# Attention, soft MoE and SoLU MLP on one core: combine weights turned four tiles at once, first w_out products in three groups

## The chip, the core and the metric

The kernel runs on one core of a Trainium2 chip. Its time is that of one execution on the device in microseconds (us); the number of a kernel is the median of its runs. A core has a matrix engine (TensorE, PE in the profile; PEld is its weight loads), VectorE (DVE), ScalarE (ACT), GpSimd (POOL) and SyncE (SP), which here issues all transfers to the 16 DMA engines. PSUM is the memory that TensorE writes to, SBUF the main memory on the core.

## The reference

Three stages on 4608 tokens in fp32: attention in chunks of 64 positions, a soft mixture of experts with 8 experts of 4 slots, and an MLP with a SoLU and a normalisation over 1024 features.

```python
scores = scale * np.matmul(q_c, k_c.transpose(0, 1, 2, 4, 3))
...                                  # softmax over the chunk
x = (attn @ v_c)                     # 4608 x 512
logits = x @ phi                     # 4608 x 32
d = softmax(logits, over tokens);  slot_input = d.T @ x
slot_out[e] = np.maximum(slot_input[e] @ w1[e], 0.0) @ w2[e]
c = softmax(logits, over slots);   x = c @ slot_out
h = x @ w_in                         # 4608 x 1024
e = np.exp(h - h_max); solu = h * e / (sum(e) + 1e-09)
ln = (solu - mu) / np.sqrt(var + 1e-06) * g_ln
return ln @ w_out                    # 4608 x 512
```

## The kernel before

The 4608 tokens are 36 tiles of 128. The program has three parts.

From 0 to about 131 us a loop of steps works through attention and the logits tile by tile; the logits of all tiles stay in `lall` (128 tokens x 36 tiles x 32 slots).

From there to about 205 us a list of named operations, `ORDER`, sets the order in which the program is written, and with it the order on each engine's queue: every engine works through its own instructions in that order, each one waiting for what it needs. Behind each name stands a small function (`op("name", "what it depends on")(function)`). `ON_VECTOR` lists the evictions and copies that run on VectorE; the others run on ScalarE. In this part come the softmax over tokens, the expert products (`w1_...` and `w2_...`, and `wc48` to `wc63` for the second half of the experts' w2, L963), the slot outputs turned (`soc`, `soct`, L1023), their product with w_in (`sw0`, `sw1`, L1084, evicted to `xb` by `pev`), and the first output tiles. The expert weights stream in beside this; all transfers stand in SP's queue, the weights in the order of use (L123, L127), and each transfer waits for the one eight before it.

Since x is c times slot_out, the kernel multiplies slot_out by w_in once (32 x 1024) and then needs for a tile only `h_ps` = the combine weights of its 128 tokens times this matrix (`h_mm`, L1272, two products of 512 columns). To keep the accuracy, each operand is split in a high and a low part: `c4T` holds for each tile 128 rows, four groups of 32 slots, the groups being high, low, high, low; `s4` holds the matrix as high, high, low, low (`s4h` casts, `s4l` subtracts).

*Combine weights.* Nine blocks of four tiles: `ch` copies a block of `lall` twice into `cc` (rounded: the high part), `cl` writes the rest beside it (L882), `ct` transposes `cc` in four products, one for each tile (L895, `c_ps`), and `ce` evicts the 128 x 512 result into `c4T` (L383 or L384). The first two tiles do without: `cpc`, `cpt`, `cpe` make fp32 transposes `cP` for them.

*First tiles.* Tile 0 (`f_` names) is handled in halves of 512 columns: `f_h0`, `f_h1` are its products (L1240), `f_m0`, `f_m1`, `f_mm` the maximum (L1206, L1209), `f_sc` a scale (L1143 to L1147), `f_e` the exponential, `f_u` the product u = h * e (L1212), `f_uh` its high part in fp16, `f_T` its transposes on TensorE (L1227), `f_Te` their evictions to `uhT`, and `f_ul` the low part (L1233), which a transposing transfer turns into `ulT` (L1236). Tile 1 has its products in `f_g0`, `f_g1`, a maximum in halves (`f_k0`, `f_k1`, `f_km`) and one exponential `f_E`. From tile 2 on a tile is whole: `Hm` (h_ps), `Hx` the maximum (L1277), `He` scale and exponential, `Av` u (L1153) with uh and its transposing transfer (L1167), `Al` ul and its transfer (L1324), `Aq` and `As` the variance.

*w_out products.* `B(i)` makes a tile's output in 24 products of 512 columns (L1345): eight uhT x w_hi, eight uhT x w_lo, eight ulT x w_hi. `B0` stands behind tile 2's h_ps and needs both halves of uhT and ulT in its list of dependencies.

From tile 2's `B` on, a loop runs over the tiles, 24 products and two h_ps products for each; h_ps has two buffers in PSUM, and tile i's is written once u of tile i - 2 has read its own.

Of the kernel before, what the change touches and what calls it, by code (L numbers as in the profile page):

```python
# [9 lines left out]
F32 = mybir.dt.float32  # L10
F32R = mybir.dt.float32r
# [8 lines left out]
NT = 36  # L20
# [16 lines left out]
ce2 ce4 ch0 ch2 ch3 ch4 ch8 cme he00 rl01 rl11 s4h0  # L37
# [9 lines left out]
cms2 cms6 px2 cms3 ht00 he00 cz1 cms4 w1_011 rl01 w2_000 cms7 ht01 px7 cms0 cz2 cz3 px3 w2_001 cz4 px6 cz5 cms5
px5 he01 w2_010 w2_011 id16 so0 px4 cms1 w1_100 sot0 px0 px1 w1_101 late ch0 cl0 px8 wmt ch2 cl2 cpc wmv ct0 ch1
w1_110 rl10 cl1 ch3 ct1 hi0 hi1 lo0 ht10 hi6 ch4 cl3 ce0 cl4 ct2 ce1 ce2 w1_111 he10 cpt cpe ch5 rl11 ct3 wc48
ht11 hi4 ce3 hi5 lo2 wc49 ct4 hi3 hi7 cl5 lo3 hi2 wc50 ch6 he11 ce4 wc51 cl6 wc52 wc53 ct6 wc54 wc55 ch8 ct5 ce6  # L50
soe0 soc0 wc56 wc57 ch7 soct0 cl7 ct7 ce5 wc58 cl8 wc59 wc60 soce0 ce7 wc61 soc2 ct8 soct2 wc62 wc63 soc3 lo1
# [11 lines left out]
def soft_moe_kernel(ctx: ExitStack, tc, qkT, v1, w12, w64, phi, g_ln, cst, out):  # L63
# [73 lines left out]
    free.extend([w_tile(ring)] * RING)  # L137
# [736 lines left out]
    cc_t = {}  # L874
# [12 lines left out]
    def combine_t(b):
        cc = cc_t[b].bitcast(F32)
        if ps3 is None:
            t = ps2.tile([128, 4, 128], F32, tag="c", name="c_ps")  # L890
        else:
            t = ps3.tile([128, 4, 128], F32, tag="uhT_ps", name="c_ps", bufs=1)
        T["c", b] = t
# [289 lines left out]
    def f_open():  # L1183
# [3 lines left out]
        for t in ("nm0", "nm1", "z0", "z1", "z3"):  # L1187
# [10 lines left out]
            ks=(4, 5, 6, 7, 0, 1, 2, 3),  # L1198
# [5 lines left out]
    def f_max(t, n):  # L1204
        x = F["hs"][n] if t == "nm0" else F["h1"][:, ts(n, 512)]
        nc.vector.tensor_reduce(out=F[t][n], in_=x, axis=AX.X, op=ALU.max, negate=True)  # L1206
# [31 lines left out]
    for n_ in range(2):  # L1238
# [5 lines left out]
        op("f_k%d" % n_, "f_g%d" % n_)(lambda n=n_: f_max("nm1", n))  # L1244
# [11 lines left out]
    op("f_km", "f_k0 f_k1")(lambda: f_min("nm1"))  # L1256
# [32 lines left out]
    op("Hm2", "f_h0 f_h1 f_g0 f_g1 s4l0 s4l1 ce0")(lambda: h_mm(2))  # L1289
# [5 lines left out]
    op("B0", "f_Te0 f_Te1 f_ul0 f_ul1 Hm2")(lambda: B(0))  # L1295
    op("Hm3", "B0 Av1")(lambda: h_mm(3))
# [42 lines left out]
    def B(i):  # L1339
        d = st[i]  # L1340
        o = ps3.tile([128, 512], F32, tag="o", name="o_ps", bufs=3)
        n = 0
        for lt, w in ((d["uhT"], w_hi), (d["uhT"], w_lo), (d["ulT"], w_hi)):
            for fc in d.get("ks", range(8)):
                nc.tensor.matmul(o, lt(fc), w(fc), start=(n == 0), stop=(n == 23))  # L1345
                n += 1
        d["o"] = o
# [105 lines left out]
```

## Time and profile before

| | us |
|---|---|
| median of 3 runs | 414.41 |
| lowest and highest run | 413.31, 415.01 |
| profiled execution, whole | 413.71 |
| its span in the trace | 411.9 |
| TensorE busy | 388.2 (94%) |
| VectorE busy | 324.2 (79%) |
| DMA, mean | 241 GB/s |

The span is what the trace shows of the profiled execution; 1.8 us of it lie around the span. Busy shares are means over three parts with different limits: the DMA engines are full in the weight stretch from about 150 to 188 us, TensorE is full in the loop over the tiles. Of the chain that ended last, 45% are the w_out products at L1345.

### The profile page before, as it was taken

What the parts mean: (1) busy time and instruction counts of PE and PEld (TensorE: products, weight loads), DVE (VectorE), ACT (ScalarE), POOL (GpSimd) and SP (SyncE); (2) the same over time, 40 slices, a digit from 0 to 9 for tenths busy, and PEclk for the clock granted to TensorE, in tenths of its full rate; (3) what the DMA queues carried; (4) which work ended last, traced back from release to release, by engine and by line L of the source; (5) the groups of instructions that cost most, each with busy time, mean ns of one, the idle gap of its engine ahead of it and who ended that gap; (6) DMA issues with size and microseconds to landing.
All of it is one profiled execution on the core that took longest, in us unless ns stands there. A gap on an engine that the chain in (4) does not pass through costs nothing.

```text
span 411.9 us, 10062 instructions
## 1 busy us (share of the span) xinstructions
PE 388.2 (94%) x3761; PEld 217.2 (53%) x3761; DVE 324.2 (79%) x790; ACT 224.6 (55%) x458; POOL 207.2 (50%) x200
## 2 busy tenths in 40 slices
PE   3899999999999899989899999999999999999997
PEld 3667767667766642335344444444444444444445
DVE  2699889989988567673889999988888888888840
ACT  2477777777776522223565555655455554554521
POOL 1477766776768428340025555544554454544430
PEclk9999999999999999999989999999999999999999
DMA  6999999999999999993045767775676665666661
GB/s 216 363 386 371 377 382 386 385 371 387 380 380 352 399 399 407 407 410 142 14 91 116 156 150 166 160 147 132 136 145 153 129 141 134 134 154 143 137 156 53
DMA packets 106884, 99.32 MB, mean 241 GB/s; under 512 B 79188, under 2 KB 79828, under 8 KB 106836
## 3 DMA queue, kind: packets, MB, share of 16 engines
q1 hardware_dynamic: 106832, 98.68, 76.9%
q8 instruction: 30, 0.49, 0.5%
q14 instruction: 22, 0.15, 0.1%
HBM read 70.60 MB, written 9.44 MB: 194 GB/s over the span
## 4 chain that ended last, share of the span: by engine, by line
PE 79%; DVE 8%; DMA 5%; ACT 3%; POOL 2%; issue 2%; SPq 1%; ACTq 0%; DVEq 0%; POOLq 0%
PE o_ps L1345 45%; PE s_ps L249 5%; PE h_ps L1272 4%; PE x_ps L275 3%; PE h_ps L912 3%; PE xt_ps L401 3%; DMA vall<-in_v 2%; PE lt_ps L304 2%; PE h_ps L963 2%; PE pt_ps L392 2%; PE h_ps L949 2%; PE sl_ps L456 1%; DMA raw<-in_w 1%; PE o_ps L1357 1%; DMA cs<-in_cst 1%
## 5 line engine op out<-in xcount | busy, mean ns | idle before, releaser
L1158 POOL TENSOR_SCALAR uh<-u,sc 128x1024 f16<-128x1024 f32 (+1 forms) x35 | 72.1, 2059 | 42.7 <-issue 31.8
L1345 PEld LDWEIGHTS <-uhT 128*128 128x128 f16 x560 | 52.5, 99 | 68.6 <-issue 11.3
L1345 PE MATMUL o_ps<-xb,uhT 128*128 128x512 f16 x280 | 67.5, 385 | 0.0
L1345 PE MATMUL o_ps<-wo,uhT 128*128 128x512 f16 x280 | 66.9, 382 | 0.0
L1345 PE MATMUL o_ps<-xb,ulT 128*128 128x512 f16 x280 | 66.2, 379 | 0.0
L1283 ACT ACTIVATE e<-h_ps,nm 128x1024 f32<-128x1024 f32 x34 | 37.8, 1113 | 47.0 <-DVE nm L1277 47.0
L1174 ACT ACTIVATE e<-u,nmean 128x1024 f32<-128x1024 f32 x35 | 40.2, 1149 | 34.9 <-DVE nmean L1173 34.9
L1277 DVE TENSOR_REDUCE nm<-h_ps 128x1 f32<-128x1024 f32 x34 | 41.5, 1221 | 12.5 <-PE h_ps L1272 12.5
L1312 POOL TENSOR_TENSOR a<-a,mhalf 128x1 f32<-128x1 f32 x36 | 20.7, 577 | 59.6 <-DVE a L1329 54.5
L249 PE MATMUL s_ps<-qk 128*64 128x128 f32 x576 | 42.1, 291 | 8.5 <-DMA qk<-in_qkT 5.2
L1153 DVE SCALAR_TENSOR_TENSOR u<-h_ps,e 128x1024 f32<-128x1024 f32 x35 | 42.9, 1225 | 6.2 <-ACT e L1283 6.2
L1322 DVE SCALAR_TENSOR_TENSOR ul<-u,sc,uh 128x1024 f16<-128x1024 f32 x35 | 45.4, 1296 | 0.0
L1345 PEld LDWEIGHTS <-ulT 128*128 128x128 f16 x280 | 27.4, 98 | 33.0
L249 PEld LDWEIGHTS s_ps<-qk 128*64 128x64 f32 x576 | 33.1, 144 | 18.9 <-issue 8.9
L258 DVE TENSOR_REDUCE mx<-s_ps 128x8 f32<-128x512 f32 x36 | 24.6, 684 | 14.2 <-PE s_ps L249 14.1
L212 POOL TENSOR_SCALAR conv<-conv 128x256 f32<-128x256 f32 x16 | 17.7, 1109 | 24.1 <-ACT conv L199 24.1
L1272 PE MATMUL h_ps<-s,c4T 128*128 128x512 f32 x68 | 27.7, 488 | 1.9 <-DVE s L1097 1.9
L383 ACT ACTIVATE xt_b<-xt_ps 128x512 f32<-128x512 f32 (+1 forms) x37 | 21.6, 585 | 13.1 <-PE xt_ps L401 12.5
L1365 ACT ACTIVATE ob<-o_ps,a 128x512 f32<-128x512 f32 x35 | 23.7, 678 | 9.0 <-PE o_ps L1345 8.0
L212 POOL TENSOR_SCALAR conv<-conv,g_sb 128x256 f32<-128x256 f32 x16 | 19.6, 1228 | 13.9 <-ACT conv L199 13.9
L383 ACT ACTIVATE pt<-pt_ps 128x512 f32<-128x512 f32 x35 | 20.8, 594 | 10.6 <-PE pt_ps L392 9.0
L270 ACT ACTIVATE p<-p 128x512 f32<-128x512 f32 x35 | 21.7, 619 | 6.6 <-DVE p L264 6.6
(226 smaller groups left out, 645.6 us busy)
## 6 DMA issues: line engine op xcount, KB each, us to landing
w<-in_w SPq DMA_DIRECT2D x48, 512.0 KB, 7.8
qk<-in_qkT SPq DMA_DIRECT2D x72, 256.0 KB, 5.8
vall<-in_v SPq DMA_DIRECT2D x36, 260.0 KB, 5.8
out<-ob SPq DMA_DIRECT2D x35, 256.0 KB, 2.1
raw<-in_w SPq DMA_DIRECT2D x32, 256.0 KB, 5.7
qk<-in_w SPq DMA_DIRECT2D x3, 512.0 KB, 6.7
w_raw<-in_w SPq DMA_DIRECT2D x4, 256.0 KB, 7.1
vall<-in_w SPq DMA_DIRECT2D x2, 512.0 KB, 8.6
```

Source lines behind the costliest of these rows:

```text
L212: nc.gpsimd.tensor_scalar(out=m, in0=m, scalar1=1.265625 * 2.0 ** -30, scalar2=g, op0=ALU.is_ge, op1=ALU.mult)
L249: nc.tensor.matmul(s[ts(c, 64), ts(g, 128)], b[:, 1, ts(2 * g + c, 64)], b[:, 0:3:2, ts(2 * g + c, 64)], start=True, stop=True, tile_posit ...
L258: mark("mx", nc.vector.tensor_reduce(out=mx, in_=s, axis=AX.X, op=ALU.max))
L383: A=lambda o, i: nc.scalar.activation(out=o, in_=i, func=AF.Copy),
L1153: nc.vector.scalar_tensor_tensor(out=u, in0=d["h"], scalar=1.0, in1=e, op0=ALU.mult, op1=ALU.mult, accum_out=zz[:, 1:2])
L1158: nc.gpsimd.tensor_scalar(out=uh[:, 0:n], in0=u[:, 0:n], scalar1=d["sc"][:, 1:2], scalar2=1.0, op0=ALU.mult, op1=ALU.mult)
L1174: nc.scalar.activation(out=d["e"], in_=d["u"], func=AF.Square, bias=nmean, scale=1.0, accum_out=d["zz"][:, 2:3])
L1272: nc.tensor.matmul(h[:, ts(n, 512)], c4T[:, i, :], s4[n], start=True, stop=True)
L1277: nc.vector.tensor_reduce(out=nm, in_=st[i]["h"], axis=AX.X, op=ALU.max, negate=True)
L1283: nc.scalar.activation(out=d["e"], in_=d["h"], func=AF.Exp, bias=d["nm"], scale=1.0, accum_out=d["zz"][:, 0:1])
L1322: nc.vector.scalar_tensor_tensor(out=ul, in0=d["u"], scalar=d["sc"][:, 1:2], in1=d["uh"], op0=ALU.mult, op1=ALU.subtract)
L1345: nc.tensor.matmul(o, lt(fc), w(fc), start=(n == 0), stop=(n == 23))
```

## The change

It has four parts.

1. The combine weights. Only tiles 2 and 3 still go through `ch`, `cl`, `ct`, `ce`, at half the width (two transposes). Tiles 4 to 35 are turned from `lall` itself, four tiles in one transpose since four tiles of 32 slots are 128 columns: `cat0` and `cat1` make four transposes each into one PSUM bank (`ca_ps`), `cah` copies them, rounded, to one spare weight buffer, `cal` subtracts and writes the rest to a second. In these the rows are (tile within four, slot), so 16 transfers (`cad`, 128 KB each) bring each quarter of 32 partitions to the four row groups of `c4T`.
2. Tile 0's w_out products are three operations: `B0` (uhT x w_hi) now ahead of the sum's cast and tile 2's h_ps, `B01` (uhT x w_lo), and `B02` (ulT x w_hi), which alone needs ulT.
3. Tile 1's maximum is one reduction over 1024 columns instead of two and a minimum.
4. `ORDER` is written anew, from the end of the attention on.

```diff
-    def combine_h(b):
-        cc_t[b] = cc = e3c.tile([128, 4, 4, 32], F32R, tag="cc", name="cc")
-        V(E("ch%d" % b))(cc[:, :, 0:4:2, :], lall[:, ts(b, 4), :].unsqueeze(2).to_broadcast([128, 4, 2, 32]))
...
-    for b in range(NB):
-        op("ch%d" % b, "cz5 late")(lambda b=b: combine_h(b))
...
+    def combine_h():
+        T["cc"] = cc = e3c.tile([128, 2, 4, 32], F32R, tag="cc", name="cc")
+        V(E("ch"))(cc[:, :, 0:4:2, :], lall[:, 2:4, :].unsqueeze(2).to_broadcast([128, 2, 2, 32]))
...
+    def many_t(q):
+        T["ca", q] = t = ps2.tile([128, 4, 128], F32, tag="c", name="ca_ps")
         for k in range(4):
...
+            nc.tensor.transpose(t[:, k, :], lall[:, ts(1 + 4 * q + k, 4), :].rearrange("p t s -> p (t s)"), ident)
+
+    def many_h(q):
+        V(E("cah%d" % q))(stage(0)[:, ts(q, 512)], T["ca", q].rearrange("p k n -> p (k n)"))
+
+    def many_l(q):
+        nc.vector.tensor_tensor(
+            out=stage(1)[:, ts(q, 512)], in0=T["ca", q].rearrange("p k n -> p (k n)"),
+            in1=stage(0).bitcast(F32)[:, ts(q, 512)], op=ALU.subtract
+        )
+
+    def many_d():
+        dst = c4T.bitcast(F32)
+        for t in range(4):
+            for r in range(4):
+                nc.sync.dma_start(
+                    out=dst[ts(r, 32), 4 + t:NT:4, :],
+                    in_=stage(r % 2).bitcast(F32)[ts(t, 32), :].rearrange("p (b n) -> p b n", b=8),
+                )
...
-            ks=(4, 5, 6, 7, 0, 1, 2, 3),
+            ks=range(8),
...
-        op("f_k%d" % n_, "f_g%d" % n_)(lambda n=n_: f_max("nm1", n))
...
-    op("f_km", "f_k0 f_k1")(lambda: f_min("nm1"))
+    op("f_km", "f_g0 f_g1")(lambda: nc.vector.tensor_reduce(out=F["nm1"][0], in_=F["h1"], axis=AX.X, op=ALU.max, negate=True))
...
-    op("B0", "f_Te0 f_Te1 f_ul0 f_ul1 Hm2")(lambda: B(0))
-    op("Hm3", "B0 Av1")(lambda: h_mm(3))
+    op("B0", "f_Te0 f_Te1")(lambda: B(0, 0, 1))
+    op("B01", "B0")(lambda: B(0, 1, 2))
+    op("B02", "B01 f_ul0 f_ul1")(lambda: B(0, 2, 3))
+    op("Hm3", "cad B02 Av1 Hm2")(lambda: h_mm(3))
```

What the new order does to the queues, at three places. On TensorE, at the end of the expert products (`h_ps_2589`, from the weights `w`, `vall` and `w_pt`), before:

```order
L963 MATMUL h_ps_2589<-w,xb_86 4x128 x16
L1023 MATMUL soc_ps<-cs,xb_85 128x128 x2
L895 MATMUL c_ps<-cs,cc 128x128 x4
L963 MATMUL h_ps_2589<-w,hTb 4x128 x16
L963 MATMUL h_ps_2589<-w,xb_86 4x128 x16
L895 MATMUL c_ps<-cs,cc 128x128 x4
L1023 MATMUL soc_ps<-cs,xb_84 128x128
L963 MATMUL h_ps_2589<-vall,hTb 4x128 x8
L963 MATMUL h_ps_2589<-w_pt,hTb 4x128 x4
L963 MATMUL h_ps_2589<-vall,hTb 4x128 x4
L1023 MATMUL soc_ps<-cs,xb_85 128x128
```

and after, from the same products on:

```order
L992 MATMUL h_ps_2603<-w,xb_86 4x128 x16
L992 MATMUL h_ps_2603<-w,hTb 4x128 x16
L992 MATMUL h_ps_2603<-w,xb_86 4x128 x16
L1052 MATMUL soc_ps<-cs,xb_85 128x128 x2
L1052 MATMUL soc_ps<-cs,xb_84 128x128
L992 MATMUL h_ps_2603<-vall,hTb 4x128 x8
L992 MATMUL h_ps_2603<-w_pt,hTb 4x128 x4
L992 MATMUL h_ps_2603<-vall,hTb 4x128 x4
L1052 MATMUL soc_ps<-cs,xb_85 128x128
```

The transposes `c_ps` of the combine weights, which stood between the groups of expert products, are gone from there; `ca_ps` stands further up, ahead of the `hTb` products.

On SP, at the end of the weights, before:

```order
L123 DMA w<-in_w 128x1024 x24
L123 DMA vall<-in_w 128x1024
L127 DMA w_pt<-in_w 128x512
L127 DMA vall<-in_w 128x512
L1236 DMA_TRANSPOSE ulT<-ul_3164 128x4x128
L1236 DMA_TRANSPOSE ulT<-ul_3163 128x4x128
L1167 DMA_TRANSPOSE uhT<-uh 128x8x128
```

and after:

```order
L122 DMA w<-in_w 128x1024 x24
L122 DMA vall<-in_w 128x1024
L126 DMA w_pt<-in_w 128x512
L126 DMA vall<-in_w 128x512
L924 DMA c4T<-w 32x8x128 x16
L1265 DMA_TRANSPOSE ulT<-ul_3122 128x4x128
L1265 DMA_TRANSPOSE ulT<-ul_3123 128x4x128
L1196 DMA_TRANSPOSE uhT<-uh 128x8x128
```

The 16 transfers of `c4T` stand behind the last weight and ahead of the first two transposing transfers of `ulT`.

On VectorE, from the maximum of tile 0 (`nm`, L1209 and L1238) to the first half of ul, before:

```order
L1209 TENSOR_TENSOR nm_3167<-nm_3167,nm_3168 128x1
L384 CAST s_3198<-ss_ps 128x512
L1143 SCALAR_TENSOR_TENSOR sc<-nm_3167 128x1
L1144 TENSOR_SCALAR sc<-sc 128x1
L1147 RECIPROCAL sc<-sc 128x1
L1212 SCALAR_TENSOR_TENSOR u_3159,z_3173<-h_ps,e_3157 128x512
L1212 SCALAR_TENSOR_TENSOR u_3160,z_3174<-h_ps,e_3158 128x512
L1206 TENSOR_REDUCE nm_3169<-h_ps 128x1
L1206 TENSOR_REDUCE nm_3170<-h_ps 128x1
L1233 SCALAR_TENSOR_TENSOR ul_3164<-u_3160,sc,uh_3162 128x512
```

and after:

```order
L1238 TENSOR_TENSOR nm_3126<-nm_3126,nm_3127 128x1
L1172 SCALAR_TENSOR_TENSOR sc<-nm_3126 128x1
L1173 TENSOR_SCALAR sc<-sc 128x1
L1176 RECIPROCAL sc<-sc 128x1
L1241 SCALAR_TENSOR_TENSOR u_3118,z_3132<-h_ps,e_3116 128x512
L384 CAST s_3160<-ss_ps 128x512
L1241 SCALAR_TENSOR_TENSOR u_3119,z_3133<-h_ps,e_3117 128x512
L1284 TENSOR_REDUCE nm_3128<-h_ps 128x1
L1262 SCALAR_TENSOR_TENSOR ul_3122<-u_3118,sc,uh_3120 128x512
```

The scale (`sc`) moves ahead of the cast of `s`, the cast between the two halves of u, and tile 1's maximum is one row.

## Rows read from the trace of the kernel before

**Rows 1.** Busy time by stretch at the seam: us, engines (x instructions), PEclk, DMA.

```profile
180.00:188.00 8.00, 7.98 (x118) 3.97 (x117) 4.43 (x12) 3.69 (x8) 0.00 (x0) 1.00 1.03 407
190.00:191.00 1.00, 1.00 (x26) 0.70 (x18) 0.00 (x0) 0.28 (x1) 0.00 (x0) 1.00 0.01 4
```

**Rows 2.** SP's timeline, 181.5 to 205 us: start, duration, queue, line, out<-in.

```profile
181.79 0.33 SPq L127 DMA_DIRECT2D vall<-in_w  x1
202.41 3.58 SPq L1236 DMA_TRANSPOSE ulT<-ul  x2
```

**Rows 3.** Transfers issued from 177 to 182.5 us: KB each, median us to landing.

```profile
vall<-in_w SPq DMA_DIRECT2D x1, 256.0 KB, 8.9
```

**Rows 4.** The chain that ended last, 185 to 224 us: start, us, what.

```profile
190.55 0.59 PE c_ps L895 x4
...
191.30 1.08 PE h_ps L963 x32
...
197.25 0.70 DVE nm L1206
...
204.53 6.88 PE o_ps L1345 x24
...
211.87 5.20 PE o_ps L1345 x24
...
217.99 5.20 PE o_ps L1345 x24
```

**Rows 5.** Timeline of the first two output tiles, all engines, 197.5 to 204.6 us.

```profile
198.10 0.69 DVE L384 CAST s<-ss_ps 128x512 fp32r<-128x512 f32 x1
...
199.17 0.69 DVE L1212 SCALAR_TENSOR_TENSOR u<-h_ps,e 128x512 f32<-128x512 f32 x1
...
200.52 0.72 ACT L1222 ACTIVATE uh<-u,sc 128x512 f16<-128x512 f32 x1 [0.90 <-DVE u L1212]
...
200.89 0.80 PE L1227 MATMUL uhT_ps<-ident,uh 128*128 128x128 f16 x8
...
201.60 0.74 DVE L1233 SCALAR_TENSOR_TENSOR ul<-u,sc,uh 128x512 f16<-128x512 f32 x1
201.73 0.60 ACT L383 ACTIVATE uhT<-uhT_ps 128x512 f16<-128x512 f16 x1
202.37 0.69 DVE L1097 TENSOR_TENSOR s<-ss_ps,s 64x512 fp32r<-64x512 f32 x1
...
203.21 0.47 PE L1272 MATMUL h_ps<-s,c4T 128*128 128x512 f32 x1 [1.52 <-DVE s L1097]
```

**Rows 6.** Busy time by stretch around the first w_out products, columns as in rows 1.

```profile
202.00:203.00 1.00, 0.00 (x0) 0.00 (x0) 0.97 (x2) 0.32 (x1) 0.00 (x0) 1.00 0.00 0
205.00:208.00 3.00, 3.00 (x9) 1.06 (x8) 2.90 (x8) 1.48 (x4) 0.69 (x1) 0.52 0.24 46
```

**Rows 7.** VectorE's timeline behind it, 204.6 to 218 us.

```profile
204.68 0.15 DVE L1143 SCALAR_TENSOR_TENSOR sc<-nm 128x1 f32<-128x1 f32 x1
...
205.25 1.23 DVE L1153 SCALAR_TENSOR_TENSOR u<-h_ps,e 128x1024 f32<-128x1024 f32 x1
...
209.50 1.21 DVE L1153 SCALAR_TENSOR_TENSOR u<-h_ps,e 128x1024 f32<-128x1024 f32 x1
...
211.90 1.23 DVE L1277 TENSOR_REDUCE nm<-h_ps 128x1 f32<-128x1024 f32 x1 [1.19 <-PE h_ps L1272]
...
215.65 1.22 DVE L1153 SCALAR_TENSOR_TENSOR u<-h_ps,e 128x1024 f32<-128x1024 f32 x1
```

**Rows 8.** Groups by line and shape, 165 to 197 us: busy, mean, idle before.

```profile
L895 PE MATMUL c_ps<-cs,cc 128*128 128x128 f32 x36 | 5.8, 285 | 1.1 <-ACT cP L383 0.5 <-DVE isw L1047 0.4 <-ACT c4T L383 0.2
...
L882 DVE TENSOR_TENSOR cc<-lall,cc 128x256 fp32r<-128x256 f32 x9 | 4.0, 466 | 2.7 <-ACT cc L383 2.6
```

**Rows 9.** Transposing transfers issued from 200 to 216 us, columns as in rows 3.

```profile
ulT<-ul SPq DMA_TRANSPOSE x4, 3.0
uhT<-uh SPq DMA_TRANSPOSE x2, 3.1
```

More of the change, by code (lines that the diff above doesn't have):

```diff
@@ L36 @@
 ON_VECTOR = """
-ce2 ce4 ch0 ch2 ch3 ch4 ch8 cme he00 rl01 rl11 s4h0
+cme he00 rl01 rl11 s4h0 ce ch
 """.split()
@@ L47 @@
[L47 to L51, printed above, removed]
@@ new lines @@
+PT351 ptev1 xT33 ev34 x350 x351 lall7 xtev33 tm7 rz35 xT34 LT33 xtev34 rc35 own_v LT34 ev350 xT350 ev351 xT351
+lte8 xtev350 xtev351 L8 LT35 px tm8 mT8 lte83 Ls mn8 L83 lall83 mnl mb lall8 own_p d8 d7 de7 de8 hz1 mc al hz0
+sl70 sl71 z8 sl80 zacc8 sl81 zt acc80 own_t acc81 zr si0 si1 siT cm0 cm1 open2 own_x w1_000 w1_001 cme cz0
+w1_010 cms2 cms3 id16 rl00 ht00 px3 he00 w1_011 cms6 w2_000 w2_001 cms7 cz1 px2 px7 rl01 cms5 cz2 cms4 ht01 he01
+px6 cz3 cz4 cz5 cms1 cms0 w2_010 px1 w2_011 px4 w1_100 so0 px5 sot0 late px0 w1_101 ch rl10 px8 cpc wmt cl cpt
@@ new lines @@
+wmv w1_110 hi0 ht10 w1_111 hi1 ct hi4 rl11 ce cpe he10 wc48 hi5 wc49 ht11 hi3 hi2 hi6 he11 cat0 lo2 cah0 cat1
+cal0 cah1 lo0 wc50 cal1 cad wc51 hi7 wc52 lo3 wc53 wc54 soe0 wc55 wc56 soc0 wc57 wc58 wc59 soc2 wc60 wc61 lo1
+soct0 soct2 soce2 wc62 wc63 soce0 soc3 soct3 soce3 sw0 sw1 pev0 pev1 end2 f_open f_h0 f_h1 f_m0 f_m1 f_mm f_e0
+f_e1 f_sc f_u0 f_g1 rp0 s4h0 f_u1 f_uh0 f_uh1 f_g0 f_T0 rp1 f_T1 f_Te1 f_Te0 f_km s4h1 B0 f_E f_ul0 f_s1 s4l0
+s4l1 Hm2 f_ul1 Av1 f_mean Hx2 B01 Al1 f_v0 He2 B02 Hm3 Av2 Aq1 Hx3 Aq2 He3 B1 As1 f_v1 Al2 As2
@@ L136, in soft_moe_kernel @@
     gone = []
-    free.extend([w_tile(ring)] * RING)
+    free_ring = [w_tile(ring)]
+    free.extend(free_ring * RING)
     xpool = pool("xb", 1)
@@ L882, in combine_l @@
+    def combine_l():
+        cc = T["cc"]
         nc.vector.tensor_tensor(
-            out=cc[:, :, 1:4:2, :], in0=lall[:, ts(b, 4), :].unsqueeze(2).to_broadcast([128, 4, 2, 32]),
+            out=cc[:, :, 1:4:2, :], in0=lall[:, 2:4, :].unsqueeze(2).to_broadcast([128, 2, 2, 32]),
             in1=cc.bitcast(F32)[:, :, 0:4:2, :], op=ALU.subtract
         )
[L887 to L893, printed above, removed]
-        for k in range(4):
-            nc.tensor.transpose(t[:, k, :], cc[:, k].rearrange("p r s -> p (r s)"), ident)
@@ L897, in combine_e, with combine_t @@
-    def combine_e(b):
-        V(E("ce%d" % b))(c4T[:, ts(b, 4), :], T["c", b])
-    for b in range(NB):
-        op("ch%d" % b, "cz5 late")(lambda b=b: combine_h(b))
-        op("cl%d" % b, "ch%d" % b)(lambda b=b: combine_l(b))
-        op("ct%d" % b, "cl%d" % b)(lambda b=b: combine_t(b))
-        op("ce%d" % b, "ct%d" % b)(lambda b=b: combine_e(b))
+    def combine_t():
+        cc = T["cc"].bitcast(F32)
+        T["c"] = t = ps2.tile([128, 2, 128], F32, tag="c", name="c_ps")
+        for k in range(2):
+            nc.tensor.transpose(t[:, k, :], cc[:, k].rearrange("p r s -> p (r s)"), ident)
@@ new lines, in combine_e, with stage @@
+    def combine_e():
+        V(E("ce"))(c4T[:, 2:4, :], T["c"])
+    op("ch", "cz5 late")(combine_h)
+    op("cl", "ch")(combine_l)
+    op("ct", "cl")(combine_t)
+    op("ce", "ct")(combine_e)
+    def stage(k):
+        if ("stage", k) not in T:
+            h = next(h for h in free if h not in gone and h is free_ring[0])
+            free.remove(h)
+            T["stage", k] = h()[0].rearrange("p k n -> p (k n)").bitcast(F32R)
+        return T["stage", k]
+    def many_t(q):
+        T["ca", q] = t = ps2.tile([128, 4, 128], F32, tag="c", name="ca_ps")
+        for k in range(4):
+            nc.tensor.transpose(t[:, k, :], lall[:, ts(1 + 4 * q + k, 4), :].rearrange("p t s -> p (t s)"), ident)
@@ L906, in soft_moe_kernel @@
+    for q in range(2):
+        op("cat%d" % q, "cz5 late")(lambda q=q: many_t(q))
+        op("cah%d" % q, "cat%d" % q)(lambda q=q: many_h(q))
+        op("cal%d" % q, "cah%d" % q)(lambda q=q: many_l(q))
+    op("cad", "cal0 cal1 late")(many_d)
     hid, hidT = {}, {}
@@ L1204, in f_max @@
     def f_max(t, n):
[L1205 removed]
+        x = F["hs"][n]
         nc.vector.tensor_reduce(out=F[t][n], in_=x, axis=AX.X, op=ALU.max, negate=True)
@@ L1337, in w_lo, with B @@
         return wlo[:, fc, :]
-    def B(i):
+    def B(i, t0=0, t1=3):
         d = st[i]
[L1341 to L1347, printed above, removed]
+        ks = d.get("ks", range(8))
+        if t0 == 0:
+            d["o"] = ps3.tile([128, 512], F32, tag="o", name="o_ps", bufs=3)
+        for t in range(t0, t1):
+            lt, w = (d["ulT"] if t == 2 else d["uhT"]), (w_lo if t == 1 else w_hi)
+            for fc in ks:
+                nc.tensor.matmul(d["o"], lt(fc), w(fc), start=(t == 0 and fc == ks[0]), stop=(t == 2 and fc == ks[-1]))
     def last_tile(i):
```

17 lines of the change are left out of this document (4 added, 13 removed).

## Prediction

> **What bounds the kernel now.** I read the busy table by stretch first, then the chain of the end, then the transfers at the seam between the two phases, then the timeline of the first output tiles.
>
> The stretch before 188 us is bound by the weight stream: from 180 to 188 the DMA engines are full (share 1.03, 407 GB/s) [rows 1]. The last of the expert weights is issued at 181.79 us [rows 2] and lands 8.9 us later [rows 3], at 190.7; between 190 and 191 the DMA share is 0.01 [rows 1]. But TensorE is behind by then. It is busy for the whole microsecond after 190 [rows 1], first with four transposes of combine weights, 0.59 us, and only then with the last 32 expert products, from 191.30 for 1.08 us, so to 192.38 [rows 4]. So the seam is 1.7 us later than the last byte, and the transposes of the combine weights are what TensorE is late by.
>
> From there a serial chain runs through the slot products to the maximum at 197.25, and a short tangle of VectorE, ScalarE and TensorE leads to the first w_out products at 204.53 [rows 4]. There the reader is to see three things. VectorE casts s at 198.10 for 0.69 us ahead of the scale and of u, which therefore starts at 199.17 [rows 5]. TensorE is idle from the end of the transposes at 201.69 [rows 5] until the first h_ps product at 203.21, which waited 1.52 us for s [rows 5], with nothing at all from 202 to 203 [rows 6]; the 24 products of tile 0 wait behind those in its order. And these 24 take 6.88 us where the next tile's take 5.20 [rows 4]: the granted clock is 0.52 from 205 to 208 [rows 6], that is the lower of its two levels (1.2 GHz) behind that hole, for a loss of 1.7 us.
>
> Behind it VectorE holds the thread. It works without a gap through the u of tile 1 (205.25) and that of tile 2 (209.50), then waits 1.19 us for the h_ps of tile 3, whose maximum starts at 211.90; u of tile 3 follows at 215.65 [rows 7]. That u frees the PSUM bank for tile 5's h_ps, and tile 2's w_out products come right after it, at 217.99 [rows 4]. From there on both kernels run the same loop, 24 products after 24 products. So what the change is worth at the end is what it moves the start of tile 2's products, and, one step ahead of that, the start of tile 3's maximum at 211.90.
>
> **The change, part by part.**
>
> *Transposes.* 36 transposes with 5.8 us of TensorE become 10; 26 x 5.8/36 = 4.2 us go. VectorE loses nine subtractions of 0.47 us [rows 8] and has three again, one of half the width and two of 128x512; the copies on VectorE and ScalarE become fewer in the same way. Each new copy or subtraction out of PSUM lies between 0.47, the subtraction of half its size, and some 0.95, twice that; a cast of 128x512 out of PSUM takes 0.69 [rows 5, 8], and I take that. They lie beside the weight stream, which runs on until 190.7 whatever they cost. Of the 4.2 us TensorE can use only what brings it to the last byte: the last product that waits for it is one of a group of 32 that takes 1.08 us, of which some 10 remain, so it ends at 190.7 + 0.35 = 191.05 instead of 192.38. **Worth 1.33 us at the seam**, and not more, as the data is the bound then.
>
> *First tile.* The chain from the seam to the maximum is the same work, so the maximum starts at 197.25 - 1.33 = 195.9. The scale now stands ahead of the cast: u's first half waits for its exponential alone and starts at 197.65 (1.52 earlier). The cast takes 0.69 between the halves, so the second half starts at 199.0, where it would have been at 198.5; this gives 0.5 back. ScalarE's uh then starts at 199.75 instead of 200.52 and the transposes end at 200.9 instead of 201.69 [rows 5]. Two copies of uhT, 0.60 each [rows 5], follow in a row, since tile 1's exponential no longer stands between them: the first w_out products can start at 202.2, against 204.53 in the chain.
>
> *Three groups.* The eight uhT x w_hi products no longer wait for s or ul. Work is neither added nor removed (24 products), only its order: eight, then tile 2's h_ps, then eight with w_lo, then eight with ulT. What VectorE must do first: u to 199.7, the one wide maximum (1.23 us as tile 3's [rows 7]; the small minimum goes) to 200.95, ul 0.74 [rows 5], three scale steps 0.57 (204.68 to 205.25 [rows 7]), s twice 0.69 [rows 5], ul 0.74: it ends at 204.4, and tile 1's u starts at 204.45 instead of 205.25 [rows 7], **0.8 earlier**. The transposed ulT lands 3.0 us after its issue [rows 9], at 207.4, so that the ulT group ends at 208.3 at full clock and tile 3's h_ps at 208.8. If the clock falls as before, the 24 products with their 6.88 us and tile 2's h_ps put this at about 210.1.
>
> *Where it ends.* VectorE's list from tile 1's u to that of tile 2 is the same as before, without gap: 0.8 earlier, the u of tile 2 starts at 208.7 to 208.9 and ends by 210.1. Tile 3's maximum then starts at about 210.2 to 210.3, by VectorE's own queue or by the slow-clocked h_ps at 210.1, whichever comes last; the two are within 0.2 us. Against 211.90 that is 1.6 earlier. From there to tile 3's u the list is the same length (one set of small steps stands earlier), so u starts at about 214.05 and tile 2's products start at about 216.3. TensorE is there in time: tile 1's products need uhT, which is issued at 206.5 and lands 3.1 later [rows 9] at 209.6, or wait for the slow clock until 210.15, and last 5.20, to 215.35. **Sum: 1.6 us**; so the wait that ends last moves from TensorE's lateness to VectorE's queue, and 0.5 to 0.6 of the first tile's 2.2 us is lost there.
>
> *The 16 transfers.* 2 MB from SBUF to SBUF, on SP behind the last weights, where nothing stood until the ulT transposes at 202.41 [rows 2]. Each waits for the one eight before it, so that half of them cannot start before 190.7. No row shows such a transfer (32 partitions, runs of 512 bytes). One bound is the weight stream's rate, 407 GB/s: 5.2 us, so to 196. The other is one that issues as a transpose does, 1.79 us each on SP (two in 3.58 [rows 2]): 16 x 1.79 = 28.6 us, to 219. I take the near end, 5 to 12 us: they are plain copies as the weights are, whose issue takes 0.33 us [rows 2] (16 x 0.33 = 5.3 us). Done by 202.5 they cost nothing: SP has no other work, the first ul is ready at 201.7, and tile 4's h_ps is not read before 215. What that hides is lost if SP or the engines are taken after 204.
>
> The Trainium skill (SBUF — State Buffer, section "Door 1: The DMA port swizzle") speaks against this layout: 32 neighbouring partitions reach only 8 of 16 ports, and it has 189 GB/s for them where 128 partitions reach 328. By it the 2 MB would take an estimated 11 us and end at about 202, just ahead of the first ulT transpose; the sum would be the same, with no reserve. No run here shows it yet.
>
> **Rivals.**
>
> *The layout comes late (slower).* The transfers hold SP or the engines; ulT and tile 1's uhT queue behind them. From 190.7 at 1.2 us each they end at 209.9; the two ulT issues (3.58) put the ulT products' end near 214.2, and tile 3's maximum 2.3 later than before, so +2.3 us, 416.7. It decides once the transfers end after about 206: two issues and the landing then reach 211.9. Against it: the weights' issue time and stream rate [rows 1, 2]. For it: short runs, quarter partitions, two waves of eight.
>
> *The last weights are slowed.* The copies are ready at about 187 and their first eight share the engines with the weights. 1 MB ahead of the last byte is 2.5 us at 407 GB/s: the seam would be at 193.5 and tile 3's maximum at 212.7, **+0.9**, 415.3. Against it: they are issued behind the weights, and the landing of 8.9 us [rows 3] looks like a queue served in order.
>
> *The hole moves.* TensorE now waits for data before 190.7. If the clock falls there as it did after 202 [rows 6], the slot products run at the lower level and lose what tile 0's lost, 1.7 us: gain about 0, 414.4. Against it: the holes are shorter than 1 us, as products keep arriving with the weights.
>
> *More than the sum.* No clock drop at all (the hole is 1.3 instead of 1.5 us) and VectorE's list is shorter in places: 2.1 to 2.6 us, about 412.0.
>
> **How the numbers follow.** The profiled execution took 413.71 us (span 411.9 and 1.8 around it); less 1.6 it is 412.1, and the span 410.3. The median of the three runs is 414.41 (413.31 to 415.01), 0.7 above the profiled one; less 1.6 it is 412.8, which I predict. Half a per cent, 2.1 us, is about what a measurement of this kernel can tell from no change, so the forecast lies within it, near its edge. Chances: the forecast 0.5 (gain 1.2 to 2.1), more than the sum 0.25, last weights slowed 0.08, hole 0.07, layout late 0.1. Some of the forecast's spread of runs falls beyond 0.5%: faster 0.32, same 0.58, slower 0.10. The range reaches from the best case (gain 3.0 with a run at the lower end) to the slowed weights: 411.4 to 415.3.
>
> **What would show it.** Right: the last expert product ends at about 191.05, with TensorE waiting for the weights ahead of it; the first w_out products start at about 202.2; the transfers have landed by 203; tile 3's maximum starts near 210.3 with VectorE not idle ahead of it for more than 0.3 us; tile 2's products start near 216.3. Wrong: a last weight landing later than 191; SP busy with the layout after 204; tile 3's h_ps after 211; a granted clock under 1 between 191 and 200.

## The result and the profile after

The changed kernel took 417.37 us (median of 6 runs, 415.78 to 419.17), the kernel before 413.65 (6 runs, 412.43 to 415.01): a ratio of 1.0092 with a 95% interval of 1.0066 to 1.0117. It is slower by 3.7 us where I had forecast 1.6 us less. The profiled execution took 417.54 us with a span of 415.7, against 413.71 and 411.9, so the two spans differ by the same 3.8 us and can be compared stretch by stretch. The ratios here and below leave out executions more than 1.5% above the fastest one of their kernel.

First the queue that carries the weights, in SP's timeline of the changed kernel (start, duration, engine, line, operation, out<-in, count):

```profile
157.19 24.81 SPq L122 DMA_DIRECT2D w<-in_w  x24
...
185.71 0.33 SPq L126 DMA_DIRECT2D vall<-in_w  x1
188.04 14.89 SPq L924 DMA_DIRECT2D c4T<-w  x16
207.11 3.72 SPq L1265 DMA_TRANSPOSE ulT<-ul  x2
```

The last weight is issued at 185.71, where [rows 2] have 181.79. The 3.9 us are lost at the other end of that queue: the first transfer into the ring of weight buffers goes out at 157.19, and SP's waits between 150 and 190 us (us in total, times, longest) say for what:

```profile
SPq L122 <- PE h_ps L941: 9.0, 7, 6.1
```

It waits 6.1 us for the first expert products of TensorE to give a buffer back. In the kernel before the same transfers start at 152.53, and the whole wait there is 1.8 us:

```profile
152.53 25.75 SPq L123 DMA_DIRECT2D w<-in_w  x24
```

```profile
SPq L123 <- PE h_ps L912: 1.8, 2, 1.2
```

Why TensorE is late there is seen in the busy table of the stretch just ahead, by the columns of [rows 1]: the changed kernel, then the kernel before.

```profile
144.00:145.00 1.00, 0.75 (x5) 0.43 (x4) 0.78 (x4) 0.21 (x2) 0.00 (x0) 1.00 1.08 418
145.00:146.00 1.00, 0.40 (x2) 0.29 (x2) 0.48 (x3) 0.12 (x1) 0.00 (x0) 0.82 0.98 385
146.00:147.00 1.00, 0.54 (x8) 0.31 (x12) 0.12 (x3) 0.90 (x3) 0.00 (x0) 0.50 1.00 397
...
156.00:160.00 4.00, 4.00 (x28) 0.81 (x24) 2.01 (x3) 0.00 (x0) 3.85 (x4) 0.59 0.45 158
```

```profile
144.00:145.00 1.00, 0.91 (x11) 0.37 (x10) 0.52 (x3) 0.42 (x2) 0.00 (x0) 1.00 1.05 414
145.00:146.00 1.00, 0.79 (x5) 0.48 (x5) 0.78 (x4) 0.24 (x2) 0.00 (x0) 1.00 1.05 406
146.00:147.00 1.00, 0.97 (x4) 0.52 (x4) 0.55 (x4) 0.85 (x3) 0.00 (x0) 1.00 1.01 397
...
156.00:160.00 4.00, 4.00 (x40) 1.17 (x36) 2.58 (x3) 0.20 (x1) 4.00 (x4) 1.00 1.03 407
```

TensorE is busy for 0.75, 0.40 and 0.54 us of the three microseconds after 144, where it was busy for 0.91, 0.79 and 0.97; the granted clock falls to its lower level (0.50, that is 1.2 GHz) in the middle of them and stays there until about 159 us. The DMA share, full in the kernel before, is 0.45 from 156 to 160. TensorE's timeline of the changed kernel gives the place (the bracket is the idle time before, and what ended it):

```profile
146.46 1.93 PE L661 MATMUL sl_ps<-xb,lt 128*32 128x256 f32 x16 [1.05 <-ACT lt L644]
...
155.27 7.30 PE L941 MATMUL h_ps<-w,xl 128*4 128x512 f32 x48
```

The products of the sum over tokens (L661) start after 1.05 us without work, behind ScalarE, and the first 48 expert products begin at 155.27 and take 7.30 us. The clock falls 0.23 us after that wait has begun (145.41) and is down for the rest of it:

```profile
145.64:146.46 0.82, 0.00 (x0) 0.00 (x1) 0.48 (x4) 0.36 (x2) 0.00 (x0) 0.50 1.01 400
```

So this one wait did not bring the clock down alone; there are smaller ones ahead of it, of 0.22 and 0.26 us. In the kernel before the expert products begin 3.8 us earlier and take 5.33:

```profile
146.27 0.70 PE L797 MATMUL cm_ps<-csum,mean_l 128*128 128x256 f32 x2
147.13 1.07 PE L661 MATMUL sl_ps<-xb,lt 128*32 128x256 f32 x16 [0.16 <-ACT lt L644]
...
151.46 5.33 PE L912 MATMUL h_ps<-w,xl 128*4 128x512 f32 x48
```

There the two products of cm0 (L797) stand in that wait, of which 0.16 us is left.

Then the end of the stream and the tail, in the chain of the changed kernel (start, us, what), against [rows 4]:

```profile
185.71 10.35 DMA vall<-in_w
...
196.10 0.65 PE h_ps L992 x8
...
197.49 2.17 PE sw_ps L1113 x16
...
211.69 3.77 DMA uhT<-uh
...
215.50 5.35 PE o_ps L1377 x24
...
221.78 5.20 PE o_ps L1377 x24
```

The last weight lands 10.35 us after its issue instead of 8.9 [rows 3], and the products that wait for it end at 196.75. Tile 2's w_out products start at 221.78, against 217.99. The 16 layout transfers are in this part of the busy table:

```profile
196.00:198.00 2.00, 1.46 (x16) 0.83 (x20) 0.17 (x1) 0.28 (x1) 0.00 (x0) 1.00 1.05 181
...
200.00:202.00 2.00, 2.00 (x6) 0.88 (x5) 1.08 (x2) 0.35 (x1) 0.00 (x0) 1.00 0.93 177
...
204.00:206.00 2.00, 1.20 (x7) 0.49 (x6) 2.00 (x6) 0.72 (x1) 0.69 (x1) 1.00 0.39 67
206.00:208.00 2.00, 0.82 (x7) 0.46 (x7) 1.92 (x6) 1.49 (x5) 0.00 (x0) 1.00 0.01 4
```

They move 177 to 181 GB/s with the DMA share near 1 after the last weight. The last of them is issued at 202.2 and lands 3.2 us later, at 205.4, so they are gone when ulT is issued at 207.11.

So the 3.8 us between the spans divide as follows, each number a difference of the rows above and of [rows 2, 4]:

| stretch | before | after | change |
|---|---|---|---|
| last weight issued | 181.79 | 185.71 | +3.92 |
| from there to the last expert product's end | 10.59 | 11.04 | +0.45 |
| from there to tile 2's w_out products | 25.61 | 25.03 | -0.58 |
| from there to the end of the span | 193.9 | 193.9 | 0.0 |

### The profile page after: what moved, and what is told of

The parts are those of the page before. It is cut to its first block, busy times and chain, and to the rows that moved or that the text cites. A ratio compares the mean times of both kernels' runs of the same rounds, so it can differ in the third digit from the quotient of the medians.

```text
span 415.7 us, 10001 instructions
## 1 busy us (share of the span) xinstructions
PE 387.3 (93%) x3735; PEld 216.1 (52%) x3735; DVE 319.5 (77%) x777; ACT 220.9 (53%) x449; POOL 206.9 (50%) x200
## 4 chain that ended last, share of the span: by engine, by line
PE 72%; DMA 11%; DVE 9%; ACT 2%; POOL 2%; issue 2%; SPq 1%; ACTq 0%; DVEq 0%; POOLq 0%
PE o_ps L1377 43%; DMA w<-in_w 6%; PE s_ps L249 6%; PE h_ps L1300 4%; PE x_ps L275 3%; PE xt_ps L401 3%; DMA vall<-in_w 2%; PE lt_ps L304 2%; PE pt_ps L392 2%; PE sl_ps L456 2%; DVE mx L258 1%; DMA cs<-in_cst 1%; PE o_ps L1387 1%; DVE p L264 1%; ACT xt_b L383 1%
## 5 line engine op out<-in xcount | busy, mean ns | idle before, releaser
L1377 PE MATMUL o_ps<-xb,uhT 128*128 128x512 f16 x280 | 66.5, 380 | 2.7 <-DMA uhT<-uh 1.5
L1342 POOL TENSOR_TENSOR a<-a,mhalf 128x1 f32<-128x1 f32 x36 | 21.8, 606 | 57.7 <-DVE a L1359 54.9
```

The lines of the kernel that those rows point to most:

```text
L1377: nc.tensor.matmul(d["o"], lt(fc), w(fc), start=(t == 0 and fc == ks[0]), stop=(t == 2 and fc == ks[-1]))
```

## The experiments

Since the time of one and the same program depends on whether TensorE's clock fell in that execution, I give for each kernel its median and, where it tells more, the mean of the executions whose mean granted clock was 0.999 or 1 ("full clock"). Of the kernel before there are 101 executions beside these experiments: 38 at full clock with a mean of 412.3 us, 61 near 0.996 with a mean of 413.8, and two lower. The 0.996 is what [rows 6] show, a fall for three microseconds at the first w_out products; where the clock fell in the executions that were not profiled is not known. "Low" below is a mean clock under 0.9935. The changed kernel was low in 6 of 6 executions, 0.983 to 0.992.

**Theories.** A: the holes near 145 us bring the clock down, and the clock holds up the weight stream. B: the layout transfers are the whole cost. C, a rival within A: not one hole, but all of the re-sequencing. To these came, after the first results, D (the tail's gain over-counted), and F against G for a transfer that lands late (an instruction fetch, or the layout transfers themselves).

### 1. The early order of before

```diff
 ORDER = """
-... the changed order up to w1_000
+... the order of before up to w1_000
```

> The changed kernel, with the operations ahead of the first expert product (w1_000) in the order of the kernel before; everything from there on as changed. Theory A (a hole on TensorE near 146 us, where the sum over tokens waits for ScalarE, brings the lower clock until 159 us; the first expert products release their weight buffers late and the weight stream stalls): granted clock 1.00 from 145 to 160, the last weight issued at about 181.8 instead of 185.7 us, and 3.3 to 3.9 us less than the changed kernel: 413.5 to 414.1. Theory B (the 16 layout transfers are what it costs, wherever they stand): no more than 0.5 us less, about 417.

Measured: median 414.43 (10 runs), ratio to the kernel before that ran beside it 1.0055 (1.0021 to 1.0088); 413.5 at full clock (4 runs), three runs low. By the medians 1.1 us of the 3.7 are left, by the ratios 2.3 of 3.8, so the early order is worth 1.5 to 2.6 us. That is more than the 0.5 us of theory B, but the two intervals overlap (experiment 3 is the clearer test), and it is less than theory A had. At full clock 1.2 us over the kernel before remain, and the clock still fell in three executions. In its profile the last weight goes out at 182.65 and lands as late as in the changed kernel:

```profile
182.65 10.40 DMA vall<-in_w
...
193.10 0.65 PE h_ps L992 x8
...
194.49 3.76 PE sw_ps L1113 x16
```

It takes 10.40 us to land. This is one of the three low executions, and its clock fell at the early place too, from 146.8 to about 150 us, although cm0 stood in its old place, no wait just ahead was longer than 0.21 us, and TensorE was busy for 1.00, 0.91 and 0.79 us of the three microseconds after 144. The fall was short and cost the stream little (DMA share 0.88 after 154):

```profile
147.00:148.00 1.00, 1.00 (x6) 0.28 (x9) 0.44 (x4) 0.84 (x5) 0.00 (x0) 0.50 1.04 391
...
154.00:156.00 2.00, 2.00 (x24) 0.55 (x20) 1.23 (x1) 0.00 (x0) 1.95 (x2) 1.00 0.88 289
```

The last row of the chain shows a second fall: the slot products take 3.76 us instead of 2.17, since TensorE had waited twice for half a microsecond for weights and its clock had fallen, 0.50 from 196 to 198:

```profile
196.00:198.00 2.00, 2.00 (x12) 0.38 (x4) 0.00 (x0) 0.60 (x1) 0.00 (x0) 0.50 0.90 178
```

### 2. One operation back, one operation away

```diff
-... lall8 own_p ... siT cm0 cm1 open2
+... lall8 cm0 own_p ... siT cm1 open2
```

> The changed kernel with one operation moved back: cm0, two small products on TensorE (0.70 us), stands again ahead of the sum over tokens instead of behind it. Theory A: cm0 alone filled the hole, so the clock stays up and the time is within 0.7 us of the run with the whole early order of before, 413.5 to 414.5. Rival C (the hole comes from the sum of the re-sequencing, ScalarE's and VectorE's queues too): the clock falls all the same, 416 to 417.4. Theory B: 417.

Measured: median 416.37 (10 runs), ratio 1.0061 (1.0035 to 1.0088), low in 7 of 10. Rival C holds for this direction: putting cm0 back shortens the wait from 1.05 to 0.42 us, and the clock falls all the same.

The other direction, in the kernel before:

```diff
-... lall8 cm0 d7 ... siT open2 cm1
+... lall8 d7 ... siT cm0 open2 cm1
```

> The kernel before with one operation moved: cm0 behind the sum over tokens, where the changed kernel has it; nothing else of the change. Theory A: the granted clock falls to about 0.5 from 147 to 158 us and the time rises by 3 to 4 us, to 416.7 to 417.7. Rival C: cm0 alone is 0.7 us of a wait that other work covers, no change, 413.7 (within 0.5). Theory B: 413.7.

Measured: median 417.15 (10 runs), ratio 1.0077 (1.0041 to 1.0113), low in 8 of 10. One operation of 0.70 us, moved behind the sum over tokens, makes the kernel before 3.2 us slower by the ratio and 3.8 by the medians, with nothing else of the change in it. In its PE timeline and busy table the same picture as above:

```profile
147.64 1.07 PE L661 MATMUL sl_ps<-xb,lt 128*32 128x256 f32 x16 [0.79 <-ACT lt L644]
```

```profile
146.00:147.00 1.00, 0.63 (x4) 0.41 (x4) 0.40 (x3) 0.73 (x3) 0.00 (x0) 1.00 0.99 391
147.00:148.00 1.00, 0.36 (x8) 0.27 (x12) 0.55 (x4) 0.84 (x5) 0.00 (x0) 1.00 1.00 383
...
150.00:152.00 2.00, 2.00 (x15) 1.32 (x7) 1.45 (x4) 0.00 (x0) 0.00 (x0) 0.50 1.04 407
...
154.00:156.00 2.00, 2.00 (x11) 0.43 (x13) 1.07 (x2) 0.00 (x0) 0.30 (x1) 0.50 0.67 249
```

The wait is 0.79 us, the clock 0.50 from 150 to 156, and the DMA share 0.67 after 154. Here the clock falls at about 149.6, 2 us after the end of the wait.

### 3. The holes filled

Nothing moved, only three small products added whose result is written over by cm0's:

```diff
+    def cfill():
...
+        nc.tensor.matmul(T["cm"][:, 0:256], mean_l.to_broadcast([128, 128]), csum[:, 0:256], start=True, stop=True)
...
-... L83 lall83 mnl mb lall8 own_p ...
+... L83 cf0 lall83 mnl mb lall8 cf1 cf2 own_p ...
```

> The changed kernel with three small products (128x256, the same as cm0, results overwritten) put into TensorE's waits between 144 and 146.5 us; no work is left out and no order changed. Theory A (the holes there bring the clock down, and the clock the rest): clock 1.00 from 145 to 160 in most runs, last weight issued at about 182, time 413 to 414.5. If the early order costs by something other than the holes on TensorE (late hand-over of buffers, late own_t and own_x), the stream still stalls at 154 us and the time stays at 416.4 to 417.5.

Measured: median 414.34 (10 runs), ratio 1.0026 (1.0002 to 1.0050), low in 1 of 10; 413.8 at full clock. Added work on TensorE makes the changed kernel 2.7 us (by the ratios) to 3.2 us (by the medians beside it) faster, and the two intervals do not overlap. Its busy table:

```profile
144.00:146.00 2.00, 1.78 (x17) 0.99 (x16) 1.22 (x6) 0.51 (x3) 0.00 (x0) 1.00 1.07 411
146.00:148.00 2.00, 2.00 (x16) 1.26 (x18) 0.59 (x4) 0.84 (x4) 0.00 (x0) 1.00 1.00 399
...
156.00:160.00 4.00, 4.00 (x40) 1.14 (x36) 2.16 (x3) 0.60 (x1) 4.00 (x4) 1.00 1.03 406
```

The clock stays up, the DMA share stays full, and the last weight goes out at 182.51. So neither the order of ScalarE's and VectorE's work nor the buffers handed over later (own_t, own_x) hold up the stream; TensorE's clock does.

### 4. The layout transfers held until the weights have landed

The early order of before, and the first layout transfer made to wait for the products wc62:

```diff
-GATE = dict()
+GATE = dict(c4="wc")
...
-... cal1 cad wc51 ... wc62 wc63
+... cal1 wc51 ... wc62 cad wc63
...
+        if m == 62:
+            mark("wc", r)
...
-                nc.sync.dma_start(
+                gated("c4", nc.sync.dma_start(
```

> As the first run of these (early order of before), with the 16 layout transfers held until the products wc62 are done, so that they can't share the engines with the last weights. If mixing with the weights cost 1.4 us of landing (10.35 us in the changed kernel against 8.9 before): the last weight lands at about 190.7 and the seam is 1 to 1.4 us earlier than in that run; the transfers then last until about 204 at the 180 GB/s of the changed kernel, and the time is 0 to 1.2 us less, 412.5 to 414. If the late end of the layout decides instead, ulT queues behind it and the time is 0.5 to 2 us more, 414.3 to 416.

Measured: median 412.75 (10 runs), ratio 0.9991 (0.9959 to 1.0022), one run low; 412.3 at full clock (6 runs), against 413.5 for the same kernel unheld. The landing of the last weight tells the two apart without any clock. The unheld one took 10.40 us (experiment 1); of the held one, the transfer issued at 180.97 (KB each, us to landing):

```profile
vall<-in_w SPq DMA_DIRECT2D x1, 256.0 KB, 9.1
```

It is 10.3 to 11.2 us in the profiles of the five unheld kernels and 8.9 to 9.1 in the five profiles of held ones, against 8.9 before. So mixing costs 1.3 us in this pair. The late layout does little harm: it is issued from 189.86 on, and its last transfer, issued at 201.0, lands 3.8 us later, at 204.8. The first ulT goes out before that, at 201.87, and takes 3.7 us to land instead of 2.5; TensorE waits 0.36 us for it. SP's timeline of the held kernel, then three rows of the timeline of all its engines, tile 0's first products, the weight loads (PEld) of those with ulT, and tile 3's maximum:

```profile
180.97 0.33 SPq L126 DMA_DIRECT2D vall<-in_w  x1
189.86 11.92 SPq L924 DMA_DIRECT2D c4T<-w  x16
```

```profile
201.69 1.90 PE L1379 MATMUL o_ps<-xb,uhT 128*128 128x512 f16 x8 [1.18 <-ACT uhT L383]
...
205.66 1.41 PEld L1379 LDWEIGHTS <-ulT 128*128 128x128 f16 x8 [0.36 <-DMA ulT<-ul]
...
209.05 1.22 DVE L1307 TENSOR_REDUCE nm<-h_ps 128x1 f32<-128x1024 f32 x1
```

### 5. The tail alone

In the kernel before, with nine blocks of combine weights and the early order as they were: only the three groups, the one maximum and the changed order from the first tile on.

```diff
-    op("B0", "f_Te0 f_Te1 f_ul0 f_ul1 Hm2")(lambda: B(0))
+    op("B0", "f_Te0 f_Te1")(lambda: B(0, 0, 1))
+    op("B01", "B0")(lambda: B(0, 1, 2))
+    op("B02", "B01 f_ul0 f_ul1")(lambda: B(0, 2, 3))
...
+    op("f_km", "f_g0 f_g1")(lambda: nc.vector.tensor_reduce(out=F["nm1"][0], in_=F["h1"], axis=AX.X, op=ALU.max, negate=True))
```

> The kernel before with the tail of the changed one alone: first tile's w_out products in three groups, second tile's maximum in one, the operations from the first tile on in the changed order; combine weights in nine blocks and everything ahead as before. Theory D (the tail's gain was over-counted: with the clock up, the kernel before loses nothing at its first w_out products, and tile 1's uhT becomes the wait that ends last): from the seam to tile 2's products about 25.0 us as in the changed kernel, against 25.6 before with the clock loss; time within 0.7 us of before, 412.6 to 414, more of its runs at clock 1.00. My prediction's own step: 0.3 us of seam-independent gain by VectorE's list; the same to the eye. A slower tail (rival: ulT behind three groups): over 414.3.

Measured: median 412.74 (10 runs), ratio 0.9995 (0.9971 to 1.0018). At full clock the mean is 412.8 (8 runs) against 412.3 for the kernel before. So the tail is no shorter at equal clock; what it does is that 8 of 10 executions keep the clock, where 38 of 101 did before. Its chain shows the wait that ends last now:

```profile
191.00 1.08 PE h_ps L963 x32
...
204.97 1.23 DVE u L1153 x2
...
207.02 3.06 DMA uhT<-uh
...
210.12 5.35 PE o_ps L1348 x24
```

Tile 1's products (210.12) follow tile 1's uhT, which lands 3.06 us after its issue. From the end of the last expert product (192.08) to tile 1's u (204.97) it is 12.89 us. In the kernel before it was 12.87 (192.38 to 205.25): VectorE's list has won nothing.

### 6. Both costs taken away, and where the rest is

The held version with two of the filler products (after L83 and after lall8):

> The early order of before, the layout transfers held behind wc62, and two of the small filler products around 145.5 us. Both costs that theory A and the mixing theory name are taken away: median 411.5 to 412.3, that is 1 to 1.8 us under before, with no run under clock 0.995. If the clock falls there by chance whatever TensorE does, as in one of ten runs of the held version without fillers: median 412.7 and single runs over 415.

Measured: median 412.05 (12 runs), ratio 0.9971 (0.9955 to 0.9987), all 12 runs at full clock. It beats both kernels, the one before by 0.3%, but at full clock its mean of 412.2 is that of the kernel before: what it gains is the executions in which the clock had fallen. Its seam is earlier, yet its chain shows where this goes:

```profile
206.51 3.77 DMA uhT<-uh
...
210.33 5.35 PE o_ps L1384 x24
```

uhT is issued 0.5 us earlier than in the tail-only kernel and lands 0.2 us later. It takes 3.77 us. So it does in all seven profiles that have the layout transfers and not yet the memsets of the next test (3.7 to 3.8 us), and it takes 3.0 to 3.1 in the three without the transfers. In all seven a packet of queue q14, kind instruction, lies within that time, in the three others none. VectorE runs 13 instructions fewer in the changed kernel (777 against 790), so a fetch that stood ahead of the transfer may now stand within it. The test gives VectorE those 13 back, 14 memsets in place of one:

```diff
-    nc.vector.memset(mhalf, -0.5)
+    for _ in range(14):
+        nc.vector.memset(mhalf, -0.5)
```

> The held and filled version with 14 tiny memsets (a 128x1 tile that already holds the value) at the very start of VectorE's list, which restores the number of instructions that VectorE had before. In the six profiles with the layout transfers tile 1's uhT lands 3.7 to 3.8 us after its issue, and one instruction-fetch packet lies within that time; in the three without them it lands after 3.0 to 3.1 us with no such packet. Theory F (the fetch of VectorE's next instructions has moved into that transfer, as its list is 14 shorter): landing 3.0 to 3.1 us, tile 1's products 0.7 us earlier, and 0.3 to 0.7 us less than without the memsets: median 411.4 to 411.8. Rival G (the layout transfers themselves leave the engines or their queues uneven): landing still 3.7 to 3.8, median 412.0 to 412.3.

> The changed kernel with the three filler products and the 14 memsets, layout transfers not held. Theory F: landing of tile 1's uhT 3.0 to 3.1 us instead of 3.73, time 0.3 to 0.7 us under the version with fillers alone (413.8 at full clock), about 413.3. Rival G: 3.7 us and 413.8. Mixing with the last weights, which is still there, keeps both over the held version by 1 us or more.

Measured: the landing is 3.05 us in the one and 3.03 in the other, as theory F has it, here in the held one:

```profile
208.07 3.05 DMA uhT<-uh
```

But the times are 412.98 (12 runs) and 415.47 (5 runs), 0.9 and 1.1 us more than without the memsets, which had run on another chip. My placing accounts for it: at the head of VectorE's list they hold up the first loads, which wait for memsets behind them, so that the first load goes out at 3.04 us instead of 1.44.

```profile
0.79 1.68 DVE L85 MEMSET mhalf<- 128x1 f32 x14 [0.79 <-PEq L1481]
2.53 1.57 DVE L161 MEMSET qk<- 128x512 f32 x3
```

So they went behind those, where VectorE is idle (15 in place of one), and ran beside the version without them on one chip:

```diff
-    nc.vector.memset(mean_l, 1.0 / 1024.0)
+    for _ in range(15):
+        nc.vector.memset(mean_l, 1.0 / 1024.0)
```

> The held and filled version with the 14 memsets put where VectorE is idle, after its first memsets, instead of ahead of them, where they delayed the first loads by 1.7 us. Theory F as before: tile 1's uhT lands 3.0 to 3.1 us after its issue, nothing else moves, and the time is 0.3 to 0.7 us under the version without memsets run beside it, 411.3 to 411.8. If the gain is eaten by the wait behind it (tile 3's u, which frees the PSUM bank): no difference, 412.0 to 412.3.

> The held and filled version once more, beside the one with the memsets, on the same chip: 411.8 to 412.3, all runs at clock 1.00, uhT of tile 1 landing 3.7 to 3.8 us after its issue.

Measured: 411.33 us with them (12 runs, ratio to before 0.9964, 0.9946 to 0.9982) and 411.81 without (12 runs, 0.9978, 0.9960 to 0.9996), uhT landing after 3.06 and 3.79 us. The difference of the means is 0.4 us with runs that spread by 2 to 3 us: the landing is shown, the gain in time is not clear of noise. The version with both, 411.33, is the fastest of all, 0.36% under the kernel before.

## Why the prediction was wrong, point by point

**The step that failed first** is one I did not write down as a term. The sum starts at "the last of the expert weights is issued at 181.79 us" and takes that as given, because "the stretch before 188 us is bound by the weight stream". But the change rewrites the order from the end of the attention on, and the stream needs its buffers back from TensorE. Near 146 us it lengthened the waits of TensorE among small products, in part by moving cm0 out of one. I costed what the change takes out from 165 us on and looked at no place of the new order ahead of that; a cover that I took for granted (the stream hides everything) was gone at half the clock. That is +3.9 us to the last weight, shown above all by experiments 2 and 3, with the clock and the stream in the same profiles.

**"The hole moves"** was a rival of mine, with the right mechanism and the wrong place: I put it at 190, priced it at 1.7 us and gave it 0.07. At 190 it came too, in one profile (slot products 3.76 instead of 2.17 us), but the holes that decided lay near 145, and its price was not the products' own loss but the stream's behind them.

**"The last weights are slowed"** came true as well. I had said against it that the transfers "are issued behind the weights" and that the queue looked served in order. What is issued behind does slow it: 10.35 us to land instead of 8.9, 1.3 us by experiment 4, about half of the 2.5 that I had priced. The Trainium skill (DMA: Bandwidth & Descriptors, section "Two DMAs through the same engine are not ordered") says that the descriptors of one queue start in order but are pipelined, which agrees with it; no run here shows the single descriptors.

**The seam.** The last product "ends at 190.7 + 0.35": from landing to end it is 0.6 to 0.7 us (196.06 to 196.75). Without the mixing, in experiment 4, the last product ends at 190.73, 9.76 after the last weight's issue, so the gain is 10.59 - 9.76 = 0.8 us, not 1.33.

**The 16 transfers.** I took 5 to 12 us; held behind the weights, in experiment 4, they take 14.9 (189.86 to 204.8), and beside the last weights 17.3 (188.04 to 205.4), so they had not landed by 203. The page of the Trainium skill that I weighed (SBUF — State Buffer, section "Door 1: The DMA port swizzle") has 189 GB/s for 32 partitions, and the trace comes near it, with 177 to 181 GB/s; the nearest rows of the profile, the weights at 407, did not. That they cost the tail nothing as long as they end before ulT was right. "The layout comes late" did not happen: ulT is issued 1.7 us after their end.

**The tail.** The order of events was right, and so was the wide maximum. In the held profile of experiment 4, whose seam is near the one that I had forecast, tile 0's first products start at 201.69 (forecast 202.2) and tile 3's maximum at 209.05 (210.3). But the sum compared it with a profile in which the clock had fallen at tile 0. By the 101 executions, if those near 0.996 all have that fall, it is worth 413.8 - 412.3 = 1.5 us and happens in some six of ten; at equal clock the tail wins nothing (experiment 5). The -0.58 of the table is of this kind too: the 1.7 us of that fall (6.88 against 5.20 [rows 4]) stand in its column of before. That the median of experiment 4, 412.75, is the 412.8 that I forecast is luck: my base was 414.41 from three runs, while the kernel before beside that experiment had 413.32, and at full clock both kernels are at 412.3. And the wait that ends last was not VectorE's queue but tile 1's uhT, which I had landing at 209.6 with time to spare.

## What to carry to other kernels

A transfer stream that is full is only bound by itself while the engine that returns its buffers keeps pace: when an order is rewritten, read every stretch that it touches, and first the places where a small product stands in a wait of TensorE, since more waiting there brought the clock down here, and that cost the stream almost four microseconds. Transfers put behind a stream on the same queue can still slow its tail (by 1.3 us here), so hold them until it has landed if they are not urgent. And before a gain is summed, look at whether the profiled execution itself contains an event that comes and goes between executions.

## What the hardware showed that I had not expected

The granted clock of one program differs between executions: 38 of 101 runs of the kernel before were at full clock, 61 near 0.996. Three kernels with the same early order as the kernel before (experiments 1, 4 and 5) were low in 5 of 30 executions, the kernel before in 2 of 101. A mean does not tell where the clock fell, and the one of the five that was profiled (experiment 1) had one fall at the early place and one at the new seam. So that the waits near 145 us matter is shown by what adding and removing them does; what decides whether the clock falls in one execution stays open. It fell 0.2 us after the start of the longest wait in the changed kernel and 2 us after its end in experiment 2. With the filler products, that order and the held layout none of 48 executions was low.

An instruction fetch goes with a longer transfer: with one packet of the instruction queue q14 in its time tile 1's uhT takes 3.7 to 3.8 us instead of 3.0 to 3.1, and 13 or 14 tiny instructions more on VectorE took both away, in three profiles of three. The test points to VectorE's own fetch; by what the packet slows the transfer was not tried. Not every such packet does it: one of queue q8 lies within the uhT transfer that the kernel before issues at 218.23, and that one lands after 3.1 us.
